# The output product of chunks 3 to 8 computed in seven products over two chunks

## The chip, the core and the metric

The kernel runs on one core of a Trainium2 chip. The metric is the device time of one execution in microseconds, from three timed runs; a further execution was profiled, and all rows below are from it. Engines are called as in the profile: PE (TensorE), DVE (VectorE), ACT (ScalarE), POOL (GpSimd), SP (SyncE, which only issues DMAs here).

## The reference

Windowed attention of 8 batches, 8 heads, 576 tokens and head size 64 (half of the heads see the last 32 keys, half every fourth of the last 128), then a feed-forward layer over all 4608 tokens:

```python
attn = exp(scores - max) / sum; x = (attn @ v) as 4608 x 512
h = x @ w_in                                   # 512 -> 2048
g = np.maximum(h, 0.0) + np.log1p(np.exp(-np.abs(h)))
return g @ w_out                               # 2048 -> 512
```

## The kernel before, in words

Tokens go in nine chunks of 512 (`CH`), the 2048 columns of the hidden layer in 16 tiles `ff` of 128, two neighbouring tiles being an ff pair `p` (eight pairs). Every fp32 operand is cut into a high part (an ACT cast) and a low part (a DVE subtraction), and a product is three matmuls: high by high, high by low, low by high. All stand at line 205, one 128x512 matmul each.

Chunks 0 to 2 are computed plainly (`h_part`, `o_part`). Chunks 3 to 8 go in three doubles `d` of two chunks. Their first layer is already done in seven products over two chunks: `combine` and `split_*` make blocks a11, a12, a22, s1 to s4 of x, `weights_of_pair` makes combined weights t1 to t4 beside b11, b21, b22, and for each pair `product` issues seven products of six matmuls into two PSUM banks `h_x` and `h_y` in turn. After each product `aside` takes the bank out: a plain copy (L1342) or an addition to an earlier sum (L1344). A product may begin when the aside two products earlier has read its bank. The sum for one tile and one chunk is a unit: Abs, Exp, Ln on ACT (L1354 to L1360), softplus on DVE (L1364), cast on ACT (L648), subtraction on DVE (L654), each 128x512. The second layer is plain: `late_o` takes one unit and adds it with three matmuls each into four banks o0 to o3, 12 matmuls for a unit, so 16 x 2 x 12 = 384 for a double, beside 8 x 7 x 6 = 336 of the first layer. The last unit of all is done in halves of 256 columns, so that its evacuation and its DMAs can begin early.

Attention of a later chunk runs beside: 28 visits of PE (`visit`, tile `sv_ps`), each followed by masking, maximum, eight Exp on ACT, division and a transposition through DRAM.

The order of instructions on each engine is made when the program is built: a list scheduler holds tasks with a cost and dependencies. PE has two lists, `first` (products of h) and `second` (output matmuls); `choose` takes a product once `upto` output tasks are done, and the other list where the wanted one is not ready. The other engines take the ready task of the least rank. `tc.keep_in_program_order` pins the outcome, so each engine works its list strictly in that order.

Of the kernel before, what the change touches and what calls it, by code (L numbers as in the profile page):

```python
# [23 lines left out]
DM, DF = 512, 2048  # L24
# [26 lines left out]
EARLY = 2  # L51
HANDED = 22
VISIT_EVERY = 14.0
# [45 lines left out]
def tile_windowed_attention_softplus_ffn(  # L99
# [16 lines left out]
    dpool = ctx.enter_context(tc.tile_pool(name="dec", bufs=3))  # L116
    psum = ctx.enter_context(tc.tile_pool(name="psum", bufs=2, space=bass.MemoryType.PSUM))

    consts = const.tile([P, P + 2 * SW], BF16, name="consts")
# [45 lines left out]
    def decode_step(ff, i, step):  # L165
        key = ff, i
        if step == 0:
            words[key] = raws[key].bitcast(I32).rearrange("p (n t) -> p n t", t=2)
            words[key] = (*(words[key][:, :, j] for j in range(2)), dpool.tile([P, DM], F32, name="a"))
# [63 lines left out]
    def scratch(shape, name, c, pr):  # L233

        if c == 0:
            tag = idle.pop(0)
        elif c == 1:
            tag = turns[name][pr % len(turns[name])]
        else:
# [4 lines left out]
    still = const.tile([P, CH], BF16, name="still")  # L244
    nc.gpsimd.memset(still, 0.0)

    def load_mask(c):
# [5 lines left out]
        masks[c] = wk.tile([P, 2 * SW], BF16, name="mask", bufs=2)  # L253
# [11 lines left out]
    x_full, ones, blocks = {}, {}, {}  # L265
# [7 lines left out]
    def split_x(c, k, low):  # L273
# [10 lines left out]
        "a11": ("xl10", "xl11"), "a12": ("xh10", "xh11"), "s2": ("w6_1", "w7_1"),  # L284
        "s3": ("w8_1", "w9_1"), "s1": ("w10_1", "w11_1"), "a22": ("w12_1", "xh00"),
        "s4": ("xh01", "xl00"),
    }

    def raw_block(d, name, kt):

        c = FIRST + 1 + 2 * d
        if name == "s1":
            if (d, kt) not in ones:
                if d == 0:
                    ones[d, kt] = const.tile([P, CH], F32, name="sums", tag=("g_x", "g_y")[kt])
                else:
                    if d not in ones:
                        ones[d] = const.tile([P, 2, CH], F32, name="sums", tag="w14_0")
                    ones[d, kt] = ones[d][:, kt]
            return ones[d, kt]  # L300
        half, k = {
            "a11": (0, 0), "s2": (0, 0), "a12": (0, 1), "s4": (0, 1),
            "a21": (1, 0), "s3": (1, 0), "a22": (1, 1),
        }[name]
        return x_half(c + half, k)[:, kt]

    def combine(d, name, kt):
# [6 lines left out]
            out=raw_block(d, name, kt), in0=raw_block(d, a, kt), in1=raw_block(d, b, kt), op=op  # L314
        ))

    def split_high(d, name, kt):
# [4 lines left out]
        pin(nc.scalar.copy(out=blocks[name][0][:, kt], in_=raw_block(d, name, kt)))  # L322

    def split_low(d, name, kt):
        high, low = blocks[name]
        pin(nc.vector.tensor_tensor(
            out=low[:, kt], in0=raw_block(d, name, kt), in1=high[:, kt].bitcast(F32),
            op=ALU.subtract,
# [298 lines left out]
    def activated(i):  # L627
        e = wk.tile([P, CH], F32, name="e")
# [11 lines left out]
    def g_tile(part, i):  # L640
        turn = i % 2 if i < len(slots) else i % 3
        return const.tile(
            [P, CH], F32R, name=f"g{part}", tag=f"g_{'xy'[part == 'l']}" if turn == 2 else f"g{part}{turn}"
        )

    def g_high(i, copy=None):
        gh = g_tile("h", i)
# [3 lines left out]
    def g_low(i):  # L651
        e, gh = ready[i]
        gl = g_tile("l", i)
# [4 lines left out]
    w_out = dram.tile([NFF, P, 2, DM], F32, name="w_out")  # L658
# [98 lines left out]
    sums, diffs, homes, thirds = {}, {}, {}, {}  # L757
# [3 lines left out]
    w_2 = dram.tile([NPAIR, P, 2, HALF], F32, name="w_2")  # L761

    def weight_sum(p, j):

        parts = wt[2 * p + j, 0].bitcast(F32)
        if p < EARLY:
            sums[p, j] = dpool.tile([P, 2, HALF], F32, name="b", tag="a")
        else:
            if j == 0:
                sums[p] = const.tile([P, 2, 2, HALF], F32, name="b", tag="x_a")  # L770
            sums[p, j] = sums[p][:, j]
        pin(nc.gpsimd.tensor_tensor(
# [968 lines left out]
```

## Time and profile before

| | before |
|---|---|
| median of 3 runs (lowest, highest) | 863.24 us (861.31, 868.94) |
| profiled execution: time, span | 866.28 us, 864.5 us |
| mean granted TensorE clock | 0.99 of full speed |
| PE, DVE, ACT, POOL busy | 98%, 65%, 63%, 7% |
| DMA | 173.87 MB, mean 201 GB/s |

The span runs from the first to the last instruction; 1.78 us of the profiled time lie outside it. Busy time of PE is of pipelined matmuls whose ends are modelled, so the distance between starts tells a matmul's cost, not its duration.

### The profile page before, as it was taken

How to read it: one execution, taken by the hardware profiler on the slowest of the kernel's cores; microseconds unless marked ns; L12 is line 12 of the kernel's file. 1: busy time of each engine (PE TensorE's matmuls, PEld its weight loads, DVE VectorE, ACT ScalarE, POOL GpSimd, SP SyncE). 2: the span in 40 equal slices, each digit the busy share in tenths (PEclk: the TensorE clock that was granted, in tenths of full speed). 3: DMA queues.
4: the chain of work that ended last, by engine and by line, in shares of the span. 5: the costliest groups of instructions: out<-in, count | busy, mean ns of one | idle time of the engine just before them, and what ended most of it. 6: DMA issues, size and time to landing. Idle time of an engine off the chain costs nothing.

```text
span 864.5 us, 20007 instructions
## 1 busy us (share of the span) xinstructions
PE 848.7 (98%) x7997; PEld 692.5 (80%) x7997; DVE 565.0 (65%) x950; ACT 548.5 (63%) x1354; POOL 59.5 (7%) x58
## 2 busy tenths in 40 slices
PE   7899989999999999999999999999999999999998
PEld 3688877888888888888888888888888888888886
DVE  5889878946464478788878646667685256556522
ACT  6888768776666576777777636777584256565521
POOL 0000000001111002245200000000000000000000
PEclk7999989999999999999999999999999999999999
DMA  7888823376886423788864875878644525662152
GB/s 254 262 264 276 289 81 132 118 247 247 282 328 223 133 88 125 244 284 272 288 218 149 266 253 176 253 245 269 207 134 157 194 101 188 177 206 74 57 193 92
DMA packets 90621, 173.87 MB, mean 201 GB/s; under 512 B 10016, under 2 KB 26528, under 8 KB 90528
## 3 DMA queue, kind: packets, MB, share of 16 engines
q1 hardware_dynamic: 90240, 172.19, 60.6%
q8 instruction: 63, 1.03, 0.5%
q10 hardware_dynamic: 288, 0.41, 0.1%
q14 instruction: 30, 0.25, 0.1%
HBM read 130.61 MB, written 41.94 MB: 200 GB/s over the span
## 4 chain that ended last, share of the span: by engine, by line
PE 89%; DMA 6%; ACT 2%; DVE 2%; issue 0%; SPq 0%; ACTq 0%
PE o_ps L205 44%; PE h_ps L205 14%; PE h_y L205 13%; PE h_x L205 13%; PE sv_ps L205 6%; DMA raw<-w 1%; DMA v<-vp 1%; DMA turned<-squares 1%; ACT s L437 1%; DMA pt<-turned 1%; DMA k<-kdl 1%; PE a_ps L205 0%; DMA mask<-cst 0%; DMA q<-qp 0%; DVE gl L654 0%
## 5 line engine op out<-in xcount | busy, mean ns | idle before, releaser
L205 PE MATMUL o_ps<-gh,t 128*128 128x512 f32 (+1 forms) x776 | 263.7, 389 | 0.0
L205 PEld LDWEIGHTS o_ps<-gh,t 128*128 128x128 f32 x776 | 145.2, 188 | 29.8
L205 PE MATMUL o_ps<-gl,t 128*128 128x512 f32 (+1 forms) x388 | 150.4, 388 | 0.2 <-DVE gl L654 0.2
L205 PE MATMUL h_ps<-xh,parts 128*128 128x512 f32 x384 | 131.7, 398 | 0.4 <-DVE e L636 0.4
L205 PE MATMUL o_ps<-gh,parts 128*128 128x512 f32 x384 | 130.3, 394 | 0.5 <-ACT ob L695 0.5
L205 PEld LDWEIGHTS o_ps<-gh,parts 128*128 128x128 f32 x384 | 72.6, 189 | 16.6 <-ACT ob L695 1.0
L205 PEld LDWEIGHTS h_ps<-xh,parts 128*128 128x128 f32 x384 | 72.6, 189 | 16.4 <-DVE e L636 0.9
L205 PEld LDWEIGHTS o_ps<-gl,t 128*128 128x128 f32 x388 | 72.9, 188 | 15.1 <-DVE gl L654 0.6
L437 ACT ACTIVATE s<-s,nm 128x64 f32<-128x64 f32 x224 | 74.8, 337 | 5.3 <-DVE nm L426 4.3
L648 ACT CAST gh<-stored 128x512 fp32r<-128x512 f32 x48 | 29.8, 621 | 72.1 <-PE o_ps L205 68.0
L205 PE MATMUL h_ps<-xl,parts 128*128 128x512 f32 x192 | 75.3, 392 | 0.0
L205 PE MATMUL o_ps<-gl,parts 128*128 128x512 f32 x192 | 75.3, 392 | 0.0
L654 DVE TENSOR_TENSOR gl<-stored,gh 128x512 fp32r<-128x512 f32 x48 | 33.0, 690 | 64.1 <-ACT gh L648 64.1
L1360 ACT ACTIVATE e<-e 128x512 f32<-128x512 f32 x96 | 60.3, 630 | 2.5
L1357 ACT ACTIVATE e<-e 128x512 f32<-128x512 f32 x96 | 60.2, 630 | 2.3
L205 PE MATMUL h_y<-s,t 128*128 128x512 f32 x216 | 55.3, 391 | 0.0
L205 PE MATMUL h_x<-s,t 128*128 128x512 f32 x216 | 55.1, 390 | 0.0
L1354 ACT ACTIVATE e<-hs 128x512 f32<-128x512 f32 x48 | 30.3, 631 | 36.2 <-DVE hs L1342 31.2
L648 ACT CAST gh<-hs 128x512 fp32r<-128x512 f32 x48 | 29.8, 621 | 36.6 <-DVE hs L1364 31.8
L636 DVE SCALAR_TENSOR_TENSOR e<-h_ps,e 128x512 f32<-128x512 f32 x48 | 32.8, 685 | 27.3 <-ACT e L1091 23.4
L205 PEld LDWEIGHTS h_y<-s,t 128*128 128x128 f32 x216 | 40.3, 188 | 8.8 <-DVE hs L1342 0.4
L205 PEld LDWEIGHTS h_x<-s,t 128*128 128x128 f32 x216 | 40.5, 188 | 8.5
(113 smaller groups left out, 1428.4 us busy)
## 6 DMA issues: line engine op xcount, KB each, us to landing
t<-w_out SPq DMA_DIRECT2D x132, 256.0 KB, 3.6
raw<-w SPq DMA_DIRECT2D x64, 256.0 KB, 4.3
v<-vp SPq DMA_DIRECT2D x28, 512.0 KB, 5.3
q<-qp SPq DMA_DIRECT2D x36, 256.0 KB, 4.2
w_out<-parts SPq DMA_DIRECT2D x16, 512.0 KB, 4.2
out_t<-ob SPq DMA_DIRECT2D x32, 256.0 KB, 3.2
t<-w SPq DMA_DIRECT2D x16, 512.0 KB, 3.8
turned_over<-w_one SPq DMA_DIRECT2D x16, 512.0 KB, 3.9
```

The source lines that it names most:

```text
L205: return tc.keep_in_program_order(nc.tensor.matmul(**kw))
L437: pin(nc.scalar.activation(out=self.blocks[:, t], in_=src, func=AF.Exp, bias=self.nm[:, t : t + 1], scale=1.0 / 8.0 if self.masked else 1. ...
L636: pin(nc.vector.scalar_tensor_tensor(out=e, in0=tiles.pop(i), scalar=0.0, in1=e, op0=ALU.max, op1=ALU.add))
L648: pin((copy or nc.scalar.copy)(out=gh, in_=ready[i]))
L654: pin(nc.vector.tensor_tensor(out=gl, in0=e, in1=gh.bitcast(F32), op=ALU.subtract))
L1354: pin(nc.scalar.activation(out=es[u], in_=ready[LATE + u], func=AF.Abs))
L1357: pin(nc.scalar.activation(out=es[u], in_=es[u], func=AF.Exp, scale=-1.0))
L1360: pin(nc.scalar.activation(out=es[u], in_=es[u], func=AF.Ln, bias=1.0))
```

## The change

The second layer of a double is now done in seven passes over all eight pairs (`PASSES`), each with one block of g (a11, a22, a12, s2, s1, s3, s4) and one combination of `w_out`. A step (`block_step`) is one pass for one pair: six matmuls into two banks. A double has 7 x 8 = 56 steps, 336 matmuls. For this, g is held in tiles of 128x1024 (`raw_g`: one of the two tiles ff of two neighbouring pairs, for one chunk): Abs, Exp, Ln and softplus work on these, DVE makes the sums s1 to s4 in place (`combine_g`), ACT and DVE cut each block into high and low (`block_high`, `block_low`) in one of two or three buffer sets; a set is refilled when the two steps that read it are done. At the end of a pass `put` moves the banks out, adding an earlier one on DVE where there is one.

Also: plain copies of the first layer's banks go from DVE to ACT (`aside`). The combined weights of both layers are made before the doubles, their sums on DVE and their differences on POOL. The weights of `w_out` are stored in DRAM as the passes want them (`w_o`) and streamed back in DMAs of 512 KB, 28 for each double. Some steps of the passes a11 and a22 are wanted among the 56 products of h by `due`; where a product is not ready, a step may come early. The last 16 steps of a double are wanted among the first products of the next one. Visits are at least 11 us apart while more than 16 are left, then 14 as before.

The core of the diff:

```diff
--- before.py
+++ after.py
+SPILL = 16
...
+DUE = 25
+APART = 3.5
...
+PASSES = (
+    ("a11", "b11", 0, True), ("a22", "t4", 1, True), ("a12", "b21", 0, False), ("s2", "t2", 1, True),
+    ("s1", "t1", 0, True), ("s3", "t3", 1, False), ("s4", "b22", 0, False),
+)
 HANDED = 22
-VISIT_EVERY = 14.0
+VISIT_EVERY = 11.0
...
+    a_tiles = [const.tile([P, DM], F32, name="a", tag=f"a{k}") for k in range(5)]
...
+    def g_set(n, dtype=F32R):
+        if (n, dtype) not in g_sets:
+            g_sets[n, dtype] = [const.tile([P, 2, CH], dtype, name="g", tag=f"g{n}{k}") for k in range(2)]
+        return g_sets[n, dtype]
...
+    def weight_sum(i, p, j):
+
+        parts = wt[2 * p + j, i].bitcast(F32)
+        sums[i, p, j] = in_turn_tile().rearrange("p (k n) -> p k n", k=2)
+        pin(nc.vector.tensor_tensor(
+            out=sums[i, p, j].rearrange("p k n -> p (k n)"), in0=parts[:, 0], in1=parts[:, 1], op=ALU.add
+        ))
...
+    def take(out, in0, in1):
+        pin(nc.gpsimd.tensor_tensor(out=out, in0=in0, in1=in1, op=ALU.subtract))
...
     def aside(dst, b, temp=None):
         if temp is None:
-            pin(nc.vector.tensor_copy(out=dst, in_=banks[b]))
+            pin(nc.scalar.copy(out=dst, in_=banks[b]))
         else:
             pin(nc.vector.tensor_tensor(out=dst, in0=banks[b], in1=temps(temp), op=ALU.add))
...
+    def late_softplus(key):
+        h = raw_g(*key)
         pin(nc.vector.scalar_tensor_tensor(
-            out=h, in0=h, scalar=0.0, in1=es.pop(u), op0=ALU.max, op1=ALU.add
+            out=h, in0=h, scalar=0.0, in1=es.pop(key), op0=ALU.max, op1=ALU.add
         ))
...
-    def late_o(u, m, half=None):
-        c, ff = uses[u]
-        gh, gl = ready[LATE + u]
-        begins, final = u % NFF == 0, u % NFF == NFF - 1
-        if begins:
-            o_ps[m] = bank(f"o_ps{m}", f"o{m}")
-        cols = slice(0, CH) if half is None else slice(half * HALF, (half + 1) * HALF)
-        ws = slice(m * P, (m + 1) * P)
-        for j, (part, gg) in enumerate(((0, gh), (0, gl), (1, gh))):
-            matmul(
-                out=o_ps[m][:, cols], lhsT=held[ff][:, part, ws], rhs=gg[:, cols],
-                start=begins and j == 0, stop=(final or u == len(uses) - 2) and j == 2,
-                skip_group_check=half is not None,
-            )
-
...
+    def combine_g(name, c):
+        a, b, op = SUMS[name]
+        pin(nc.vector.tensor_tensor(
+            out=raw_g(c, *PLACE[name]), in0=raw_g(c, *PLACE[a]), in1=raw_g(c, *PLACE[b]), op=op
+        ))
+
+    def block_high(k, name, c):
+        pin(nc.scalar.copy(out=set_of(k)[0], in_=raw_g(c, *PLACE[name])))
+
+    def block_low(k, name, c):
+        high, low = set_of(k)
+        pin(nc.vector.tensor_tensor(
+            out=low, in0=raw_g(c, *PLACE[name]), in1=high.bitcast(F32), op=ALU.subtract
+        ))
+
+    def set_of(k):
+        return blocks["s4"] if k == 2 else g_set(k)
+
+    obank = {}
...
+    def block_step(d, i, p, k):
+        x, w, b, begins = PASSES[i]
+        gh, gl = (part[:, p % 2] for part in set_of(k))
+        tile_of = stream[d, i, p // 2]
+        for m in range(2):
+            if begins and p == 0:
+                obank[b, m] = bank(f"o_ps{2 * b + m}", f"o{2 * b + m}")
+            for j, (part, gg) in enumerate(((0, gh), (0, gl), (1, gh))):
+                matmul(
+                    out=obank[b, m], lhsT=tile_of[:, p % 2, part, m * P : (m + 1) * P], rhs=gg,
+                    start=begins and p == 0 and j == 0, stop=p == NPAIR - 1 and j == 2,
+                    skip_group_check=not begins,
+                )
+
...
+    def put(name, m, b, other=None):
+        dst = held_tile(name, m)
+        if other is None:
+            pin(nc.scalar.copy(out=dst, in_=obank[b, m]))
+        else:
+            pin(nc.vector.tensor_tensor(out=dst, in0=obank[b, m], in1=held_tile(other, m), op=ALU.add))
...
+    in_turn = [(i, c) for c in range(COUPLES) for i in (0, 1)]
+    in_turn += [(i, c) for i in range(2, len(PASSES)) for c in range(COUPLES)]
+
+    def due(d, n):
+
+        return sum(14 * c + DUE + APART * j <= n for c in range(3) for j in range(4))
...
+                n = len(steps) * p + k
+                base = given + 2 * len(in_turn) * d
+                if d == 0:
+                    task.upto = min(base, given - 2 * NKT + n)
+                else:
+                    task.upto = base - SPILL + min(n, SPILL)
+                task.upto += due(d, n)
...
+                at_n = len(steps) * (NPAIR * d + p) + k
+                task.deps.append(asides.get(at_n - 2) or plus_done[46 + k])
...
+                mine = asides[at_n] = Task(
+                    f"aside {d} {p} {k}", ACT if temp is None else DVE, 0.62 if temp is None else 0.70,
+                    emit, [task, before],
+                )
...
+            k = (turn - 8) % 3 if 7 < turn < 20 else turn % 2
...
+            high = Task(f"high {d} {x} {c}", ACT, 1.07, lambda k=k, x=x, c=c: block_high(k, x, c), [raw, *set_deps])
+            low = Task(f"low {d} {x} {c}", DVE, 1.24, lambda k=k, x=x, c=c: block_low(k, x, c), [high])
+            block_done[d, x, c] = low
+            for p in (2 * c, 2 * c + 1):
+                step = Task(
+                    f"step {d} {x} {p}", PE, 6 * MM, lambda d=d, i=i, p=p, k=k: block_step(d, i, p, k),
+                    [low, Landed((d, i, c))],
+                )
...
```

How the order moves, at three places. In the rows, h_x and h_y are the banks of the first layer, o_ps those of the second, a_ and s_ the blocks of x, t the weights.

PE among the products of the second double, before: after each product come output matmuls, three to a bank.

```order
L205 MATMUL h_x<-s_4282,t_3507 128x512
L205 MATMUL h_x<-s_4283,t_3507 128x512
L205 MATMUL h_x<-s_4282,t_3507 128x512 x2
L205 MATMUL h_x<-s_4283,t_3507 128x512
L205 MATMUL h_x<-s_4282,t_3507 128x512
L205 MATMUL o_ps_6931<-gh,t 128x512
L205 MATMUL o_ps_6931<-gl,t 128x512
L205 MATMUL o_ps_6931<-gh,t 128x512
L205 MATMUL o_ps_6956<-gh,t 128x512
L205 MATMUL o_ps_6956<-gl,t 128x512
L205 MATMUL o_ps_6956<-gh,t 128x512
```

The same place after the change: two products stand behind each other, and a step comes after them.

```order
L233 MATMUL h_x<-s_4420,t 128x512
L233 MATMUL h_x<-s_4421,t 128x512
L233 MATMUL h_x<-s_4420,t 128x512 x2
L233 MATMUL h_x<-s_4421,t 128x512
L233 MATMUL h_x<-s_4420,t 128x512
L233 MATMUL h_y<-a_4378,t 128x512
L233 MATMUL h_y<-a_4379,t 128x512
L233 MATMUL h_y<-a_4378,t 128x512 x2
L233 MATMUL h_y<-a_4379,t 128x512
L233 MATMUL h_y<-a_4378,t 128x512
L233 MATMUL o_ps_6765<-g,t 128x512 x3
L233 MATMUL o_ps_6769<-g,t 128x512 x3
```

What moved: the next product into a bank now often has one product between it and the last one into that bank, and nothing else.

DVE among the products of the first double, before: rows L1344 and L1342 take a bank out, and what stands between them is 128x512.

```order
L1364 SCALAR_TENSOR_TENSOR hs<-hs,e 128x512
L1344 TENSOR_TENSOR stored<-h_x,temps 128x512
L654 TENSOR_TENSOR gl<-hs,gh 128x512
L1344 TENSOR_TENSOR stored<-h_y,temps 128x512
L1364 SCALAR_TENSOR_TENSOR stored<-stored,e 128x512
L1344 TENSOR_TENSOR hs<-h_x,temps 128x512
L1364 SCALAR_TENSOR_TENSOR stored<-stored,e 128x512
L1342 COPY temps<-h_y 128x512
L1364 SCALAR_TENSOR_TENSOR hs<-hs,e 128x512
```

After, where L1376 takes a bank out, L1397 is softplus and L1412 a sum of g:

```order
L1376 TENSOR_TENSOR stored<-h_x,temps 128x512
L1397 SCALAR_TENSOR_TENSOR stored<-stored,e 128x1024 x2
L1412 TENSOR_TENSOR stored<-stored 128x1024
L1376 TENSOR_TENSOR temps<-h_x,temps 128x512
L1412 TENSOR_TENSOR stored<-stored 128x1024 x2
L1376 TENSOR_TENSOR a<-h_x,temps 128x512
L1376 TENSOR_TENSOR stored<-h_y,a 128x512
L1397 SCALAR_TENSOR_TENSOR stored<-stored,e 128x1024
L1376 TENSOR_TENSOR stored<-h_x,temps 128x512
```

What moved: instructions of 128x1024 now stand ahead of rows that take a bank out.

DVE between the products of the first double and those of the second, where PE works on the second layer, before: the low parts of the stored units and one group of attention.

```order
L449 TENSOR_SCALAR sm<-sm 128x8
L452 RECIPROCAL ri<-sm 128x8
L455 TENSOR_TENSOR s<-s,ri 128x512
L654 TENSOR_TENSOR gl<-stored,gh 128x512
L477 STREAM_TRANSPOSE squares<-s 128x512
L654 TENSOR_TENSOR gl<-stored,gh 128x512 x4
L415 SCALAR_TENSOR_TENSOR s<-sv_ps,mask 128x512
L426 TENSOR_REDUCE nm<-s 128x8
```

After, at the same place (L1421 a low part of g, L1459 a bank of a pass):

```order
L1412 TENSOR_TENSOR stored<-stored 128x1024
L1421 TENSOR_TENSOR s_4550<-stored,s_4549 128x1024
L1421 TENSOR_TENSOR g<-stored,g 128x1024
L1459 TENSOR_TENSOR a<-o_ps_4957,ob 128x512
L1397 SCALAR_TENSOR_TENSOR stored<-stored,e 128x1024
L1459 TENSOR_TENSOR a<-o_ps_4961,ob 128x512
L468 TENSOR_SCALAR sm<-sm 128x8
L471 RECIPROCAL ri<-sm 128x8
L474 TENSOR_TENSOR s<-s,ri 128x512
L496 STREAM_TRANSPOSE squares<-s 128x512
L1421 TENSOR_TENSOR g<-stored,g 128x1024 x2
```

What moved: softplus and the sums of the last pairs, low parts of 128x1024 and additions out of the banks now stand here together.

## Rows read from the trace of the kernel before

**Rows 1.** The page's first part: busy time of an engine (share of the span), instructions.

```profile
PE 848.7 (98%) x7997; PEld 692.5 (80%) x7997; DVE 565.0 (65%) x950; ACT 548.5 (63%) x1354; POOL 59.5 (7%) x58
```

**Rows 2.** Stretches of the span: length, then busy time (and instructions) of PE, PEld, DVE, ACT and POOL, granted clock, DMA share, GB/s.

```profile
225.00:250.00 25.00, 25.00 (x231) 20.58 (x230) 14.03 (x25) 17.54 (x55) 1.70 (x1) 1.00 0.93 313
...
400.00:425.00 25.00, 25.00 (x229) 20.30 (x228) 21.69 (x34) 17.23 (x45) 13.71 (x12) 1.00 0.83 284
...
440.00:466.00 26.00, 26.00 (x235) 21.43 (x234) 23.04 (x39) 21.70 (x50) 0.00 (x0) 1.00 0.47 145
...
600.00:625.00 25.00, 24.53 (x195) 20.21 (x189) 17.76 (x28) 14.93 (x37) 0.00 (x0) 1.00 0.69 204
```

**Rows 3.** The waits of PE: who waited for whom, us in total, times, longest.

```profile
PE sv_ps L205 <- DMA pt<-turned: 3.0, 3, 1.4
...
PE o_ps L205 <- DVE gl L654: 0.2, 1, 0.2
```

**Rows 4.** The chain of work that ended last, in order of time: start, us, what.

```profile
602.13 2.78 ACT s L437 x16
...
661.92 40.80 PE o_ps L205 x180
```

**Rows 5.** Groups by line and form on PE: the output matmuls of the doubles (busy us, mean ns of one, idle before).

```profile
L205 PE MATMUL o_ps<-gh,t 128*128 128x512 f32 x760 | 260.8, 391 | 0.0
L205 PE MATMUL o_ps<-gl,t 128*128 128x512 f32 x380 | 148.1, 390 | 0.2 <-DVE gl L654 0.2
```

**Rows 6.** Groups by line and form on DVE (busy us, mean ns of one, idle before): low part and softplus of a stored unit, a plain aside, and the one form of 128x1024.

```profile
L654 DVE TENSOR_TENSOR gl<-stored,gh 128x512 fp32r<-128x512 f32 x48 | 33.0, 690 | 64.1 <-ACT gh L648 64.1
L1364 DVE SCALAR_TENSOR_TENSOR stored<-stored,e 128x512 f32<-128x512 f32 x48 | 32.9, 690 | 3.2 <-ACT e L1360 3.1
...
L1342 DVE COPY hs<-h_x 128x512 f32<-128x512 f32 x12 | 8.3, 691 | 5.9 <-PE h_x L205 5.4
...
L277 DVE TENSOR_TENSOR xl<-x_full,xh 128x1024 fp32r<-128x1024 f32 x2 | 2.3, 1201 | 0.0
```

**Rows 7.** The same view for ACT: one pass of Exp, a copy out of a PSUM bank, the one form of 128x1024.

```profile
L1357 ACT ACTIVATE e<-e 128x512 f32<-128x512 f32 x96 | 60.2, 630 | 2.3
...
L1116 ACT COPY ob<-o_ps 128x512 f32<-128x512 f32 x12 | 7.0, 586 | 12.1 <-PE o_ps L205 12.0
...
L281 ACT CAST xh<-x_full 128x1024 fp32r<-128x1024 f32 x2 | 2.1, 1040 | 0.0
```

**Rows 8.** The same view for POOL: a difference of combined weights.

```profile
L780 POOL TENSOR_TENSOR t<-b 128x256 f32<-128x256 f32 x8 | 7.5, 934 | 4.4 <-DVE a L326 2.9 <-DVE t L792 1.0
```

**Rows 9.** Timeline of DVE where nothing is waited for: start us, duration us, line, operation.

```profile
465.18 0.68 DVE L326 TENSOR_TENSOR s<-sums,s 128x512 fp32r<-128x512 f32 x1
465.79 0.68 DVE L326 TENSOR_TENSOR a<-x_full,a 128x512 fp32r<-128x512 f32 x1
466.39 0.68 DVE L654 TENSOR_TENSOR gl<-hs,gh 128x512 fp32r<-128x512 f32 x1
```

**Rows 10.** Timeline of PE and DVE where the kernel before has four products behind each other: the first three, and the aside of the first.

```profile
656.32 1.52 PE L205 MATMUL h_x<-a,turned_over 128*128 128x512 f32 x6
...
657.67 1.52 PE L205 MATMUL h_y<-s,t 128*128 128x512 f32 x6
...
657.88 0.69 DVE L1342 COPY hs<-h_x 128x512 f32<-128x512 f32 x1
...
659.03 1.52 PE L205 MATMUL h_x<-s,t 128*128 128x512 f32 x6
```

**Rows 11.** Timeline of POOL and DVE where both work on tiles in SBUF.

```profile
387.56 2.51 POOL L772 TENSOR_TENSOR b<-parts 128x512 f32<-128x512 f32 x2 [2.50 <-DVE parts L792]
...
388.84 1.79 DVE L1364 SCALAR_TENSOR_TENSOR hs<-hs,e 128x512 f32<-128x512 f32 x1
```

**Rows 12.** Stretches with the columns of rows 2, around PE's longest pause after the opening, and one of much DMA before it.

```profile
100.00:106.00 6.00, 6.00 (x29) 4.95 (x27) 5.77 (x11) 3.99 (x9) 1.52 (x1) 1.00 1.03 381
...
114.00:116.00 2.00, 2.00 (x31) 1.74 (x28) 1.09 (x2) 0.00 (x0) 0.00 (x0) 0.50 0.58 146
116.00:118.00 2.00, 2.00 (x6) 1.52 (x6) 1.93 (x5) 0.28 (x1) 0.00 (x0) 0.50 0.62 236
118.00:120.00 2.00, 2.00 (x7) 1.57 (x6) 0.74 (x2) 1.94 (x4) 0.00 (x0) 0.60 0.00 0
```

**Rows 13.** Timeline of PE: the waits of that pause, and the longest one after it, in brackets.

```profile
111.25 0.30 PE L205 MATMUL sv_ps<-pt,v 64*64 64x32 f32 x4 [1.12 <-DMA pt<-turned]
...
112.91 1.92 PE L205 MATMUL sv_ps<-pt,v 64*64 64x32 f32 x60 [1.36 <-DMA pt<-turned]
...
615.69 1.12 PE L205 MATMUL sv_ps<-pt,v 64*64 64x32 f32 x60 [0.47 <-DMA pt<-turned]
```

**Rows 14.** The end of the timeline: the last evacuation and the last DMA (its issue).

```profile
860.66 0.42 DVE L1616 COPY pt<-o_ps 128x256 f32<-128x256 f32 x1 [0.29 <-PE o_ps L205]
...
861.12 0.34 SPq L1622 DMA_DIRECT2D out_t<-pt  x1
```

**Rows 15.** The page's part on DMA issues: count, KB each, median us from issue to landing.

```profile
out_t<-ob SPq DMA_DIRECT2D x32, 256.0 KB, 3.2
```

More of the change, by code (lines that the diff above doesn't have):

```diff
@@ L788, in high_part, with weight_24 @@
+    def weight_24(i, p):
+        d, one, two = diffs[i, p], sums[i, p, 0], sums[i, p, 1]
+        take(two[:, 1], two[:, 1], d[:, 0])
+        b21 = one[:, 1] if i == 0 else two[:, 0]
+        take(b21 if i == 0 and p < RESIDENT else two[:, 0], b21, two[:, 1])
     def high_part(high, low, src):
@@ new lines, in tile_windowed_attention_softplus_ffn, with feed @@
+    stream, spare, tag_of = {}, [], {}
+    saved = set()
+    wanted = []
+    def feed(tag):
+        spare.append(tag)
+        begun = []
+        while spare and (key := wanted[0]()) is not None:
+            d, p, what = key
+            assert key in saved or all((*key, j) in saved for j in range(2)), key
+            tag_of[key] = spare.pop(0)
+            tile_of = stream[key] = const.tile([P, 2, 2, HALF], F32R, name="t", tag=tag_of[key])
+            if what == "2":
+                load_dma(out=tile_of[:, 0].bitcast(F32), in_=w_2[p])
+                begun.append((key, 0.256))
+                continue
+            src = {
+                "one": lambda: w_one[p].rearrange("p a (b n) -> p a b n", b=2),
+                "two": lambda: w_two[p].rearrange("p a (b n) -> p a b n", b=2),
+                "13": lambda: w_13[p],
+            }.get(what, lambda: w_o[p, what])()
+            load_dma(out=tile_of.bitcast(F32), in_=src)
+            begun.append((key, 0.512))
+        return begun
@@ L881, in add_buffer @@
[L881 to L893 removed]
+        both = home(p) if d == 0 and p < RESIDENT else tile_of
@@ L895, in visit @@
+        return [[both[:, part, h, k * P : (k + 1) * P] for k in range(2)] for part in range(2)]
     def visit(n, alone=False):
@@ L1014, in open @@
                 self.after <= t + 1e-9
[L1015 removed]
+                and all(
+                    d.over(t + LATENCY * (getattr(d, "engine", PE) == self.engine != PE)) for d in self.deps
+                )
                 and all(ring.open(t) for ring, _ in self.takes)
@@ new lines, in run @@
+    def run(task, t, engine=PE):
+        for ring, until in task.takes:
+            ring.take(until)
+        task.emit()
+        cost = task.cost
+        if engine == DVE and cost > 0.40 and not task.name.startswith(FROM_PSUM):
+            cost += min(max(free_at[POOL] - t, 0.0), SHARED)
+        if task.engine == SP:
+            free_at[SP] = t + 0.08
+            task.end = arrival(t, task.cost)
+        else:
+            free_at[task.engine] = t + cost
+            task.end = t + cost + LATENCY + 0.2 * (task.engine == PE)
+        heapq.heappush(ends, task.end)
+        heapq.heappush(ends, free_at[task.engine])
+        if engine in queues:
+            queues[engine].remove(task)
```

1092 lines of the change are left out of this document (558 added, 534 removed), and 4 rows, old and new, of the table s3.

## The prediction

> **What bounds the kernel now.** I read the page's first part first [rows 1]: PE is busy for 98% of the span, DVE and ACT for about two thirds, POOL for 7%. A mean over stages can hide a stage with another limit, so the stretches come next [rows 2]: while DMA is at 93%, while POOL works for 55% of the stretch and DVE for 21.69 of 25 us, and while DVE (23.04 of 26) and ACT are both loaded, PE has no idle time. Then the waits of PE [rows 3]: the largest group from 8 us to the end is 3.0 us, for attention's data, and the output matmuls waited 0.2 us in all. The chain of waits agrees [rows 4]: its long links are PE's own work, 180 output matmuls in 40.80 us, so 0.2267 us for one matmul. Work taken off PE therefore shortens the kernel, as long as what replaces it keeps clear of PE.
>
> **What PE saves.** The trace has 760 + 380 output matmuls of the doubles [rows 5], and 24 halves that count as 12: 1152. After the change there are 3 x 56 x 6 = 1008. Products of h (1008) and visits (28) stay. So 144 matmuls go, 144 x 0.2267 = 32.6 us, if PE is as full as before.
>
> **What the other engines get.** Counted from the order, priced by rows. DVE [rows 6]: 48 plain asides leave (48 x 0.69 = -33); 96 softplus of 0.69 become 48 of 1.20 (-9); 96 low parts of 0.69 become 84 of 1.20 (+34); 48 sums of g come (+58), 36 additions out of banks (+25); weight sums move here from POOL (32 x 0.69, +22), and low parts of weights add some 10; plain evacuations that leave give -7. Together about +98: 565 + 98 = 663 us, 79% of a span of 841. The form of 128x1024 is priced by its one row, 1.20. ACT [rows 7]: 48 copies at 0.586 (+28), casts of 84 x 1.04 for 96 x 0.63 (+27), Abs, Exp and Ln on 1024 columns instead of twice 512 (144 x (1.04 - 1.26) = -32), weight casts a few: about +30, 578 us, 69%. POOL: 64 differences at 0.93 [rows 8], 60 us, all ahead of the doubles' products. No engine is full on average; what matters is what stands behind what, since each works its list strictly in order.
>
> One thing decides how full DVE is. Where nothing is waited for, instructions that last 0.68 begin 0.61 and 0.60 apart [rows 9], so durations overcount its load by about a tenth. The Trainium skill, "VectorE: DVE Perf Modes", section on the DRAIN, says that the next instruction does not start until the pipe of the one before is empty; these starts disagree, though the same section allows that an instruction not held by a wait begins earlier. If the rule held throughout, DVE's load would be the durations in full; that is rival 2, worked out from rows.
>
> **Asides behind long instructions.** A product may begin once the aside two products earlier has read its bank. In the order, products whose predecessor into the same bank stands two back, with only one product between, go from 4 to 54 (the second excerpt of the order shows such a place). The row for this [rows 10]: products start 1.35 apart; the aside of the first ran from 657.88 to 658.57, 0.46 before the third product started into its bank. So an aside may be 0.46 late free of charge. In 25 of the 54 it stands directly behind a 128x1024 instruction (17 on DVE, 8 on ACT). If that has just begun, the aside comes 1.20 late and the product waits 0.74; if it is nearly over, nothing. With the moment of arrival evenly spread over the 1.20, the mean wait is 0.74 x 0.74 / (2 x 1.20) = 0.23 us. **25 x 0.23 = 5.7 us**, between 0 and 25 x 0.74 = 18.5. Behind a waiting product stands all of PE, its steps included.
>
> **POOL.** A softplus that ran beside a POOL sum took 1.79 instead of 0.69 [rows 11], so removing that work beside the doubles gives DVE some time, which nothing waited for: 0. The differences now beside the weights' preparation also slow DVE there; PE was full in such a stretch (400 to 425 in [rows 2]), so 0, at most 3.
>
> **DMA.** The order has 193 MB instead of 172. The heaviest intervals between visits carry 7232 KB in 21.2 us of matmuls (349 GB/s) and 5952 KB in 18.5 (330). Such rates have been met: 381 GB/s over 6 us with PE full [rows 12], and 313 over 25. I cost them at 0, upper end 5. Visits 11 us apart instead of 14 spread the same matmuls otherwise: 0.
>
> **Between the products of two doubles.** Here PE works steps only, and DVE must make low parts (1.20), puts, the last softplus and sums, and attention. By durations DVE has 57.7 us of this after the first double, in 240 matmuls and 3 visits of 2.0 (60.4 us of PE), and 54.3 in 58.4 after the second; by spacing a tenth less. It fits, with 2.7 to 8 us to spare. With 89% as the most DVE has shown beside a full PE (23.04 of 26 [rows 2]), it would need 65.1 and 61.3, so 7.6 us too much: the upper end. A set's refill takes 1.04 + 1.20 in sequence, 2.28 with gaps; two steps on another set cover 12 x 0.2267 = 2.72, and twice that where three sets turn. At the handover from pair 7's products to the steps that need them, ACT has seven instructions of 1.05, two casts of 1.04, eight Exp in 2.78 [rows 4], a copy of 0.59; with an aside and a low part 14.9 us, against ten products and a visit, 15.6. That is 0.7 to spare, three times. I take **2.0 us** for the stretches together, nearer to 0 because durations themselves still fit.
>
> A pause can cost more than itself. After PE waited 1.12 and 1.36 for a transposition [rows 13], the granted clock stood at 0.50, 0.50 and 0.60 in the next three stretches of 2 us [rows 12], 1.2 of 2.4 GHz: some 2.7 us lost on top. A pause of 0.47 [rows 13] left the stretch around it at 1.00 [rows 2]. My waits are of the second size, so no clock term. The Trainium skill, "TensorE: Matmul & The Clock Gate", also has an idle array at the lower rate until it has been busy again; this trace agrees, and by it short waits in sequence could add what rival 3 counts.
>
> **The end.** Before, the last half bank took 0.42 on DVE and its DMA began 0.04 later, 3.4 before the end [rows 14]. Now a whole bank is added (0.69) and 256 KB go out, whose landing took 3.2 in the median [rows 15]. **+1.1**, between 0.5 and 2.
>
> **Sum**, against the profiled span: 864.5 - 32.6 + 5.7 + 2.0 + 1.1 = 840.7. With 1.78 around it 842.5, beside 866.28 before. That execution is 3.04 above the median of the runs, so the median becomes 839.4, rounded to 839. With its own bounds (asides 0 to 12, stretches 0 to 5) this case runs from 832 to 848.
>
> **Rivals.** 1. All covered: DVE's starts as close as in [rows 9] everywhere and asides arriving in good time. 864.5 - 32.6 + 0.5 = 832.4, median 831. For it: PE lost 0.2 us at output matmuls so far. Against: 25 asides did not stand behind 1.20 before.
> 2. DVE bounds the step stretches, and DMA its busiest intervals: 7.6 for 2.0 and 3 for DMA, so 840.7 + 5.6 + 3 = 849.3, median 848. For it: each figure of DVE counted in durations leaves under 3 us. Against: the spacing.
> 3. Within 1%: the handovers, only 0.7 us to spare, become pauses of 2.5 us as large as that of [rows 13], each with 2.7 at half clock: 3 x 5.2 = 15.6, median 855. Against: ACT's chain there would have to slip by over 3 us, past the 0.7 to spare.
> 4. Slower: in the products DVE and ACT run a backlog, so that an aside always meets a 128x1024 instruction just begun. Each of the 54 tight products then waits 0.74, 40.0 in place of 5.7: median 874. It decides against the change from 40 of the 54 on (839.4 - 5.7 + 40 x 0.74 = 863.3). The order speaks against: only 25 stand directly behind one.
>
> **How the numbers follow.** About 1%, 8.6 us, can be told from no change here. Chances: the forecast 0.42, rival 1 0.20, rival 2 0.20, rival 3 0.11, rival 4 0.07. Faster by over 1% (under 854.6): 0.82; within 1%: 0.11; slower: 0.07. The range for 8 in 10 goes from 830, just under rival 1, to 854, over rival 2.
>
> **What the changed profile would show.** 1008 output matmuls of the doubles, a long run of them still 0.227 apart; else the saving is wrong. PE's waits behind products named by DVE or ACT lines of asides, some 6 us together, mostly under 0.74 each; none is rival 1, 40 is rival 4. DVE near 663 us and ACT near 578; waits of output matmuls for low parts in the step stretches about 2 us; more with DVE full there is rival 2. Stretches of granted clock under 1.00 in the doubles would be rival 3. Wrong altogether I would be if PE waited for streamed weights, which I cost at 0, or if a 128x1024 instruction of DVE took much over 1.20.

## The result, and the profile after

| | before | after |
|---|---|---|
| median of the runs (lowest, highest) | 864.51 us (861.31, 868.94; 4 runs, the profiled one among them) | 838.12 us (837.28, 839.28; 4 runs) |
| ratio to before, 95% interval | | 0.9692 [0.9645, 0.9740] |
| profiled execution: time, span | 866.28, 864.5 us | 839.28, 837.5 us |

The kernel is faster by 3.1%, within the stated range and 1 us from the forecast. A second set of six runs gave 838.55 us and 0.9691 [0.9656, 0.9727]. Three executions in the sets below, one of the kernel before and one each of the kernels with plain asides on DVE and with softplus in halves, ran at a mean granted clock of 0.59 to 0.85 and are left out of all medians and ratios.

The page's first part, to be read against [rows 1]: PE lost 33.5 us of busy time, DVE gained 89, ACT 29. PE is still the one engine without room on average.

```profile
PE 815.2 (97%) x7839; PEld 664.1 (79%) x7841; DVE 654.0 (78%) x923; ACT 577.6 (69%) x1235; POOL 63.6 (8%) x74
```

Groups by line and form on PE and then on DVE (busy us, mean ns of one, idle before). The second layer of the doubles is now 864 + 144 = 1008 matmuls where the kernel before had 1152 (the 1140 of [rows 5], and 24 halves that count as 12). The new forms of 128x1024 on DVE take 1.22 us, against 1.20 of the one row there was [rows 6].

```profile
L233 PE MATMUL o_ps<-g,t 128*128 128x512 f32 x864 | 209.4, 390 | 0.6 <-DVE g L1421 0.5
...
L233 PE MATMUL o_ps<-s,t 128*128 128x512 f32 x144 | 34.9, 390 | 0.0
```

```profile
L1421 DVE TENSOR_TENSOR g<-stored,g 128x1024 fp32r<-128x1024 f32 x72 | 87.7, 1220 | 33.2 <-ACT g L1417 32.9
L1412 DVE TENSOR_TENSOR stored<-stored 128x1024 f32<-128x1024 f32 x48 | 58.3, 1218 | 0.5
L1397 DVE SCALAR_TENSOR_TENSOR stored<-stored,e 128x1024 f32<-128x1024 f32 x48 | 58.2, 1216 | 2.5 <-ACT e L1393 2.4
```

To see where time went, both spans are cut where the first product of h starts. The two stretches of the kernel before, then of the one after (length, then busy time and instructions of PE, PEld, DVE, ACT and POOL, granted clock, DMA share, GB/s):

```profile
0.00:332.72 332.72, 321.45 (x3945) 257.63 (x3946) 232.85 (x423) 234.23 (x652) 25.95 (x28) 0.97 0.64 211
332.72:864.50 531.78, 527.27 (x4053) 434.85 (x4051) 332.15 (x529) 314.26 (x702) 33.56 (x30) 1.00 0.60 195
```

```profile
0.00:334.48 334.48, 317.81 (x3815) 255.89 (x3818) 262.55 (x464) 244.64 (x669) 63.55 (x74) 0.97 0.76 251
334.48:837.50 503.02, 497.43 (x4025) 408.26 (x4023) 391.40 (x460) 332.92 (x567) 0.00 (x0) 1.00 0.68 221
```

The second stretch is 28.8 us shorter. One visit moved into it from the first (128 matmuls of the small kind, 1.9 us), so 30.7 are gained there of the 32.6 of the 144 matmuls. The first stretch is 1.8 us longer, and 3.7 with the visit that left it. The second stretch came out the same in the second profile of this kernel, 503.15; the first one 332.35. In what follows "from the first product on" is this second stretch; 5.6 of its 503.0 us are idle on PE.

The waits of PE (us in total, times, longest):

```profile
PE sv_ps L233 <- DMA pt<-turned: 5.6, 5, 3.2
...
PE o_ps L233 <- DVE g L1421: 0.5, 1, 0.5
```

No wait for an aside is in that list, and none for streamed weights. Why no aside was late shows in the timelines of PE and DVE at the tightest place of the whole program:

```profile
704.50 1.52 PE L233 MATMUL h_x<-s,t 128*128 128x512 f32 x6
705.86 1.52 PE L233 MATMUL h_y<-a,t 128*128 128x512 f32 x6
707.22 1.52 PE L233 MATMUL h_x<-s,t 128*128 128x512 f32 x6
708.58 1.59 PE L233 MATMUL h_y<-a,t 128*128 128x512 f32 x6
```

```profile
706.06 0.69 DVE L1376 TENSOR_TENSOR stored<-h_x,a 128x512 f32<-128x512 f32 x1 [0.52 <-PE h_x L233]
706.67 1.22 DVE L1397 SCALAR_TENSOR_TENSOR stored<-stored,e 128x1024 f32<-128x1024 f32 x1
707.80 0.69 DVE L1376 TENSOR_TENSOR stored<-h_y,temps 128x512 f32<-128x512 f32 x1
```

The product into h_y starts at 705.86, the next into h_y at 708.58. The aside between stands behind a softplus of 1.22, begins at 707.80 and ends at 708.49, 0.09 before it is needed. A product that does have to wait starts about 0.06 behind its aside (366.95 and 367.01 in a run below), so only some 0.03 was left. The aside ahead of the softplus, at 706.06, had waited 0.52 for PE: DVE was there first. Over all 54 tight products, 46 asides end 0.46 us or more ahead of the product that waits for them, as the one of [rows 10] that nothing held up; 8 are held up by 0.04 to 0.37 (seven behind a 128x1024 instruction, one behind a 128x512 one of attention), and the smallest margin is this 0.09. One such narrow place is nothing new: the kernel before had a product that started 0.06 behind its aside, although output matmuls stood between its products.

```profile
421.48 0.68 DVE L1342 COPY hs<-h_y 128x512 f32<-128x512 f32 x1
...
422.22 1.65 PE L205 MATMUL h_y<-s,t 128*128 128x512 f32 x6
```

The end: the last two banks are evacuated together, and 3.4 us pass from there to the end of the span, as before [rows 14].

```profile
832.76 1.37 DVE L1459 TENSOR_TENSOR ob<-o_ps,ob 128x512 f32<-128x512 f32 x2 [2.45 <-PE o_ps L233]
```

### The profile page after: what moved, and what is told of

Same layout as the page of the kernel before. It is cut to its first block, busy times and chain, and to the rows that moved or that the text cites. A ratio compares the mean times of both kernels' runs of the same rounds, so it can differ in the third digit from the quotient of the medians.

```text
span 837.5 us, 19536 instructions
## 1 busy us (share of the span) xinstructions
PE 815.2 (97%) x7839; PEld 664.1 (79%) x7841; DVE 654.0 (78%) x923; ACT 577.6 (69%) x1235; POOL 63.6 (8%) x74
## 4 chain that ended last, share of the span: by engine, by line
PE 80%; DMA 7%; DVE 7%; ACT 4%; issue 1%; SPq 1%; ACTq 0%
PE o_ps L233 36%; PE h_x L233 13%; PE h_y L233 13%; PE h_ps L233 11%; PE sv_ps L233 5%; DMA pt<-turned 2%; ACT s L456 2%; DMA v<-vp 1%; DMA turned<-squares 1%; DMA q<-qp 1%; DVE a L217 1%; SPq L168 1%; DVE a L212 1%; DMA k<-kdl 1%; DMA raw<-w 1%
## 5 line engine op out<-in xcount | busy, mean ns | idle before, releaser
L233 PE MATMUL o_ps<-g,t 128*128 128x512 f32 x864 | 209.4, 390 | 0.6 <-DVE g L1421 0.5
L233 PEld LDWEIGHTS o_ps<-g,t 128*128 128x128 f32 x864 | 161.5, 188 | 35.2 <-DVE g L1421 1.6
L233 PE MATMUL o_ps<-g,parts 128*128 128x512 f32 x576 | 142.3, 393 | 0.7 <-ACT ob L707 0.6
L233 PEld LDWEIGHTS o_ps<-g,parts 128*128 128x128 f32 x576 | 107.1, 188 | 24.2 <-ACT ob L707 1.5
L1417 ACT CAST g<-stored 128x1024 fp32r<-128x1024 f32 x72 | 75.5, 1050 | 62.3 <-PE o_ps L233 55.6
L1421 DVE TENSOR_TENSOR g<-stored,g 128x1024 fp32r<-128x1024 f32 x72 | 87.7, 1220 | 33.2 <-ACT g L1417 32.9
L785 POOL TENSOR_TENSOR a<-a 128x256 f32<-128x256 f32 x64 | 56.9, 897 | 99.0 <-DVE a L780 83.4
L1397 DVE SCALAR_TENSOR_TENSOR stored<-stored,e 128x1024 f32<-128x1024 f32 x48 | 58.2, 1216 | 2.5 <-ACT e L1393 2.4
L1412 DVE TENSOR_TENSOR stored<-stored 128x1024 f32<-128x1024 f32 x48 | 58.3, 1218 | 0.5
L1390 ACT ACTIVATE e<-e 128x1024 f32<-128x1024 f32 x48 | 50.8, 1057 | 0.9
L1393 ACT ACTIVATE e<-e 128x1024 f32<-128x1024 f32 x48 | 50.6, 1059 | 1.0
```

What stands on the lines that cost most here:

```text
L233: return tc.keep_in_program_order(nc.tensor.matmul(**kw))
L785: pin(nc.gpsimd.tensor_tensor(out=out, in0=in0, in1=in1, op=ALU.subtract))
L1390: pin(nc.scalar.activation(out=es[key], in_=es[key], func=AF.Exp, scale=-1.0))
L1393: pin(nc.scalar.activation(out=es[key], in_=es[key], func=AF.Ln, bias=1.0))
L1397: pin(nc.vector.scalar_tensor_tensor(out=h, in0=h, scalar=0.0, in1=es.pop(key), op0=ALU.max, op1=ALU.add))
L1412: pin(nc.vector.tensor_tensor(out=raw_g(c, *PLACE[name]), in0=raw_g(c, *PLACE[a]), in1=raw_g(c, *PLACE[b]), op=op))
```

## The experiments

Two theories. A: PE alone sets the time, and what was gained is the 144 matmuls. B: DVE and ACT now stand so close behind PE that the order decides how much of the gain is kept. Ratios are to the kernel before on the same chip; the changed kernel has 0.969, and 1% is 8.6 us. The runs with a cost of 1.40 and with later visits had the changed kernel beside them on their chip; elsewhere two ratios are compared, each known to 2 to 5 us.

**More and fewer matmuls in the steps, in the same order.** A fourth matmul, low by low, in three of the seven passes:

```diff
+            parts = ((0, gh), (0, gl), (1, gl), (1, gh)) if i in (2, 3, 4) else ((0, gh), (0, gl), (1, gh))
```

> 144 matmuls more: a fourth matmul (low by low) for each bank in the steps of the passes a12, s2 and s1, in the order of the changed kernel otherwise. Theory, PE alone sets the time of the doubles and the 144 matmuls that the change took away are what it gained: 144 x 0.2267 = 32.6 us back, 870 to 872 us. Rival, DVE or ACT set the step stretches behind a PE that looks busy: there they gain time from longer steps, and less than 25 us come back.

865.95 us, ratio 1.0009 [0.9981, 1.0037]; from the first product on 534.70 us, 31.7 more than 503.02. There the whole gain is given back: A holds in this direction. The total missed the 870 to 872 of the theory; by the ratios 27.4 us came back, so that the total alone does not exclude the rival's 25. The difference lies ahead of the cut, where the order of both kernels is the same: this execution reached the first product of h at 330.10, the changed kernel's at 334.48. Then two matmuls instead of three in the same passes:

```diff
+            parts = ((0, gh), (0, gl)) if i in (2, 3, 4) else ((0, gh), (0, gl), (1, gh))
```

> 144 matmuls less: the steps of the passes a12, s2 and s1 leave out low weights by high g, so the output is less exact; order otherwise as in the changed kernel. Theory, PE alone bounds and the others have room: 32.6 us less, about 805. Rival, DVE is next close behind: after the first two doubles it has 57.7 and 54.3 us of work by durations where PE would then have 49.5 and 47.5, so 8.2 and 6.8 us of the 32.6 are not had and the time is about 820, with PE waiting for low parts of g.

819.78 us, ratio 0.9500 [0.9447, 0.9553]; from the first product on 489.64, only 13.4 less (16.6 in the total, by the ratios). The rival's 820 came out. The waits of PE name the engine, DVE with its low parts of g, where the changed kernel has 0.5 us:

```profile
PE o_ps L233 <- DVE g L1421: 10.4, 12, 1.8
...
PE o_ps L233 <- DVE s L1421: 1.5, 2, 1.3
```

In one of the stretches behind the second double's products (columns as above), DVE is busy without a gap and PE is not:

```profile
630.00:640.00 10.00, 8.23 (x32) 6.01 (x31) 10.00 (x11) 6.28 (x8) 0.00 (x0) 0.89 0.67 232
```

So with this order the changed kernel stands just short of the point at which DVE takes over: from the first product on, 32.6 us more on PE show nearly in full, 32.6 us less at 41%. The scheduler still counted six matmuls for the shortened steps. An order made for four was not tried, so how much of the missing 59% is DVE's load and how much the unfitting order is not separated.

**The same work, planned with wrong durations.** Only the cost that the scheduler is told changes, for DVE's and ACT's 128x1024 instructions of the doubles:

```diff
-Task(f"plus {name}", DVE, 1.24, ...)
+Task(f"plus {name}", DVE, 0.62, ...)
-Task(f"low {d} {x} {c}", DVE, 1.24, ...)
+Task(f"low {d} {x} {c}", DVE, 0.62, ...)
```

(and the sums, casts, Abs, Exp and Ln alike).

> The same work, but the list scheduler is told half the cost for each 128x1024 instruction of the doubles (0.62 and 0.54 to 0.58 instead of 1.24 and 1.07 to 1.16), so that it no longer knows which aside a long instruction will hold up. Theory, it is the order made with true costs that keeps the asides clear: PE now waits for asides, 3 to 18 us in all, 841 to 856. Rival, ACT and DVE simply have time to spare, in whatever order: within 1.5 us of 838.

909.46 us, ratio 1.0526 [1.0478, 1.0573]: slower than the kernel before, with the very instructions of the changed kernel, and far outside what either side expected. From the first product on 575.86 us, 72.8 more. The stretches and the waits of this kernel split that:

```profile
332.44:908.30 575.86, 524.52 (x4025) 411.23 (x4023) 393.58 (x460) 332.99 (x567) 0.00 (x0) 0.98 0.60 193
```

```profile
PE o_ps L233 <- DVE g L1421: 11.6, 8, 2.4
PE h_y L233 <- DVE temps L1376: 9.1, 7, 1.9
PE h_x L233 <- DVE a L1376: 5.5, 4, 1.7
PE h_x L233 <- ACT temps L1374: 5.1, 3, 2.1
PE h_y L233 <- DVE a L1376: 4.2, 4, 2.4
```

PE is idle for 575.86 - 524.52 = 51.3 us instead of 5.6, and its 4025 matmuls are busy 27.1 us longer. The first is mostly waits for low parts and asides (lines L1374, L1376). Of the second, the mean granted clock of 0.98 instead of 1.00 accounts for some 12 us (575.86 x 0.02). A matmul counts as busy for 0.39 us where the next can follow after 0.2267, so each of 43 waits in the list may hide up to 0.16 more; that estimate gives some 6 us, and the rest is not placed. One such wait, in ACT's timeline: a cast, Abs, Exp, Ln and the next Abs stand in front of a plain copy that PE needs.

```profile
364.48 1.06 ACT L1393 ACTIVATE e<-e 128x1024 f32<-128x1024 f32 x1
365.44 1.04 ACT L1387 ACTIVATE e<-stored 128x1024 f32<-128x1024 f32 x1
366.39 0.56 ACT L1374 COPY temps<-h_x 128x512 f32<-128x512 f32 x1
```

The copy ends at 366.95, and PE's product starts at 367.01 after 2.06 us of waiting. This is B, and stronger than I had put it: DVE and ACT have 22 and 31% of their time free in the changed kernel, yet an order made without true durations loses the whole gain and 45 us more. Too high a cost, 1.40 for DVE's 1.22, was tried too:

```diff
-Task(f"plus {name}", DVE, 1.24, ...)
+Task(f"plus {name}", DVE, 1.40, ...)
```

(and the low parts and sums alike).

> The scheduler is told 1.40 instead of 1.24 for each 128x1024 DVE instruction of the doubles (they take 1.22). Theory, asides are clear already and a margin moves little: within 2 us of the changed kernel. Rival, the order is so sensitive that a planner off by 13% loses several us, as being off by half lost 71: 4 us or more slower.

845.71 us, ratio 0.9777 [0.9750, 0.9804]: 7 us slower than the changed kernel beside it, the rival's result. The waits that are new are 4.1 us for low parts and a cast of g, each behind the last products of a double.

```profile
PE o_ps L233 <- DVE g L1421: 2.5, 3, 1.0
PE o_ps L233 <- ACT g L1417: 1.6, 1, 1.6
```

**No steps among the products.**

```diff
-SPILL = 16
+SPILL = 0
-DUE = 25
+DUE = 1000
```

> No step of a pass is wanted among the products of h any more (due never adds one, and the last 16 steps of a double are no longer kept for the next one); the scheduler may still take one where a product is not ready. Theory, mixing is what gives ACT and DVE the time to keep up with seven products a pair: in products alone ACT has about 80 us in 86 of PE for a double, and PE waits now and then for an aside: 3 to 8 us slower than the changed kernel, 841 to 846. Rival, mixing is worth nothing because the lists have room anyway: within 1.5 us of 838.

844.10 us, ratio 0.9766 [0.9721, 0.9811], about 6 us slower. From the first product on 511.32, 8.3 more; PE waited for low parts of g seven times, 3.5 us in all, and for asides four times, 1.1 us in all. The theory's size is right; its place only in part, since the low parts lost more than the asides, and some 3.7 of the 8.3 are not placed.

**Two buffer sets throughout.**

```diff
-k = (turn - 8) % 3 if 7 < turn < 20 else turn % 2
+k = turn % 2
```

> Two buffer sets for the blocks of g throughout, where turns 8 to 19 of a double had three. Theory, a refill of 1.04 + 1.20 behind another instruction of 1.20 on DVE is later than the 2.72 us of two steps by 0.76, and half of the 36 blocks meet one: 8 to 16 us slower, PE waiting for low parts of g. Rival, the refill of 2.28 fits in 2.72 and the third set is a luxury: within 1.5 us of 838.

843.99 us, ratio 0.9770 [0.9743, 0.9798]: about 6 us slower, less than the 8 to 16 of the theory. From the first product on 507.68, 4.7 more, of which waits for low parts are 1.9 in four pieces. So fewer refills than half were late, and the rest of the loss is not placed.

**Parts of the change undone on DVE, ACT and POOL.** Plain asides on DVE again:

```diff
-pin(nc.scalar.copy(out=dst, in_=banks[b]))
+pin(nc.vector.tensor_copy(out=dst, in_=banks[b]))
```

> The 48 plain copies out of the first layer's banks go back from ACT to DVE (+33 us on DVE, -28 on ACT), the order made anew with that known. Theory, the order keeps asides clear as long as DVE is not full in the products: within 3 us of 838. Rival, DVE at 78% is so near its bound that 4% more show: 5 to 15 us slower, with PE waiting for asides.

845.59 us (three runs), ratio 0.9801 [0.9752, 0.9850]: 9 us slower by the ratio, the rival's size. No trace that can be compared shows where it waited; the cause stays open. Softplus in two halves, planned with 1.38 instead of 1.24:

```diff
-out=h, in0=h, scalar=0.0, in1=es.pop(key), op0=ALU.max, op1=ALU.add
+out=h[:, j], in0=h[:, j], scalar=0.0, in1=e[:, j], op0=ALU.max, op1=ALU.add
```

> Softplus of the doubles in two instructions of 128x512 instead of one of 128x1024 (48 x (2 x 0.69 - 1.22) = 8 us more on DVE by durations), Abs, Exp and Ln still on 1024 columns. Theory, DVE has just enough room in the step stretches: within 2 us of 838. Rival, DVE is what bounds them already: 3 to 6 us slower.

840.03 us (three runs), ratio 0.9739 [0.9702, 0.9776]: 4 us slower by the ratio, at the edge of what can be told; from the first product on 509.45, 6.4 more. PE waited 2.3 us for low parts (0.5 in the changed kernel) and 0.4 for a cast, and its granted clock fell for a while at 448 (last section). Sums of the combined weights back on POOL:

```diff
-a = Task(f"sum0 {name}", DVE, 0.70, ...)
+a = Task(f"sum0 {name}", POOL, 1.6, ...)
```

> The 32 sums of combined weights go from DVE back to POOL (POOL +49 us, DVE -22), all before or early in the first double. Theory, nothing of that stage is on the path: within 1.5 us of 838. Rival, DVE's instructions beside POOL take up to 1.79 instead of 0.69 and the weights come later: 3 to 8 us slower.

844.97 us, ratio 0.9783 [0.9745, 0.9820]: 8 us slower. From the first product on 505.02, only 2.0 more; the rest is lost before. The first product of h itself waited:

```profile
PE h_x L233 <- DVE e L655: 3.9, 1, 3.9
```

It needs a bank that a plain softplus reads. DVE came to that at 338.64, behind four low parts of weights that it began at 333.64, after POOL's last four differences (329.35 to 332.43), and two instructions for x. Before these low parts DVE stood idle for 3.2 us, up to 331.09, for attention's Exp on ACT; the changed kernel fills that wait with its own last four low parts (324.93 to 327.42), whose differences are ready by then. So the rival's size came, and by POOL's lateness and the order made around it more than by slower DVE instructions; that is read from these times and was not tested by itself.

For the last five runs (no steps among the products, two sets, and the three here) the order was made anew. The run with 1.40 lost 7 us by a new order alone, with the same instructions. So how much of the 4 to 9 us lost here belongs to what was undone, and how much to an order that merely came out less well, these runs do not separate.

**Later visits.** After the change the largest wait on PE is for attention's data. The scheduler was told that it comes later:

```diff
             task.end = arrival(t, task.cost)
+            if task.name.startswith("bring"):
+                task.end += 4.0 if t < 30.0 else 1.0
```

The control beside it, the changed kernel:

> The changed kernel once more, beside the three others of this set. All theories: 838 within 2 us, 0.969 of the kernel before. If it comes out near 842, the differences of a few us that other runs showed against it are the spread from one chip to the next.

838.55 us, ratio 0.9691 [0.9656, 0.9727].

> The scheduler is told that a transposed block comes back from DRAM 1.0 us later than it thought, and the first one of the stage 4.0 us later, so that PE works longer on other products before a visit. Theory, the waits for this data (5.6 us in the changed kernel, with a granted clock of half behind the longest) can be filled: 3 to 6 us faster than the changed kernel beside it. Rival, later visits make the blocks of x later in turn and the wait only moves: within 1.5 us of it, or slower.

855.69 us, ratio 0.9892 [0.9862, 0.9921]: 17 us slower. The wait wasn't even filled, and a longer one came:

```profile
PE h_y L233 <- ACT s L342: 7.7, 1, 7.7
PE o_ps L233 <- DVE g L1423: 4.3, 5, 1.3
PE sv_ps L233 <- DMA pt<-turned: 3.2, 1, 3.2
```

The rival holds: later visits make the blocks of x for the first double later, and its second product waits 7.7 us for s, with the granted clock at 0.63 and 0.86 in the two stretches of 10 us from 340 on. With 2.0 and 6.0:

> As the run before, with 2.0 and 6.0 us. Theory, nothing is left to fill beyond the 3.2 us of the longest wait: the same as with 1.0 and 4.0 within 1.5 us. Rival, 28 visits a us later each starve the second double of x: 3 us or more slower than with 1.0 and 4.0.

853.51 us, ratio 0.9875 [0.9841, 0.9908], within the uncertainty of the run before: the long wait at 113 us is gone, but s is 10.3 us late. Neither of the two beat the changed kernel.

## Why the prediction was right, step by step

**What PE saves: right.** 1008 matmuls are there, the stretch from the first product on is 30.7 us shorter than its visits account for, and 144 matmuls put back cost 31.7. The 0.2267 us of [rows 4] was the right price.

**Asides behind long instructions: the term that failed.** I took 5.7 us, from an arrival "evenly spread over the 1.20". It was 0. The 54 tight products and the long instructions ahead of asides are as counted, but the arrival is not random: the order is made with durations close to the true ones, so that the long instruction has mostly ended when PE's bank is full (the 0.52 us for which DVE waited at 706.06, the 0.09 left at 708.49). The run with halved costs shows that the mechanism itself is real, some 30 us in waits for asides, so it is the order that keeps the term at 0 and not free time on DVE. The 25 asides directly behind a 128x1024 instruction are in the trace, 17 on DVE and 8 on ACT; seven were held up, by at most 0.37, where 0.46 were free. Rival 4 was this mechanism; what I said against it, that only 25 asides stand directly behind one, was not the reason that it stayed away.

**Between the products of two doubles: right, at the low end.** 0.5 us of waits for low parts against 2.0 of 0 to 7.6. Durations did fit. Beside a full PE, DVE now reaches 19.17 of 20 us, past the 89% that I had used as an upper bound:

```profile
620.00:640.00 20.00, 20.00 (x209) 16.47 (x208) 19.17 (x21) 17.50 (x34) 0.00 (x0) 1.00 0.73 212
```

In the run with fewer matmuls it had no gap from 630 to 640, and PE waited. Rival 2 was thus near in the engine it named and wrong for this kernel's time.

**The end: 1.1 taken, about 0.2 measured.** From the last matmuls' modelled end to the end of the span are 4.1 us (833.40 to 837.5) against 3.9 before (860.63 to 864.5). Larger banks and DMAs cost little there.

**DMA: right at 0.** There is no wait for streamed weights in this kernel (three of the kernels with another order have 0.3 to 0.7 us). The first row has 349 GB/s beside a full PE, while the combined weights are made; the weights of the passes stream in from 348.84 on, and the second row is of such a stretch:

```profile
300.00:320.00 20.00, 20.00 (x209) 16.49 (x208) 16.07 (x27) 13.53 (x35) 9.52 (x12) 1.00 0.96 349
517.00:538.00 21.00, 21.00 (x213) 17.29 (x212) 14.29 (x20) 17.08 (x32) 0.00 (x0) 1.00 0.88 315
```

**Visits: 0 was too low.** The order built with 14 instead of 11 us between visits is the same row for row, so that this edit alone does nothing. But visits' data was late more often: 5.6 us of waits instead of 3.0 [rows 3], 0.9 of it at 450, in the second stretch, where the kernel before had 0.5 [rows 13]. The wait at about 112 us took 3.2 and 0.5 us here against 1.1 and 1.4 before [rows 13]. The time of the first product of h varies: 327.4 to 335.2 us in profiles of kernels whose order is the same up to there (fewer matmuls, two sets), so how much of the 3.7 us lost in the first stretch belongs to the change stays open.

So the 1 us between forecast and result is partly luck. With the asides at 0, the stretches at 0.5 and the end at 0.2 the sum would be 832.6 in place of 840.7, rival 1's figure; the 837.5 measured has 3.7 us more before the first product and 0.4 more at visits, which I had costed at nothing, and 0.8 not placed. The mechanism was rival 1's, the total the forecast's. **DVE** was put at 663 us (its terms as listed add up to 100, not 98) and took 654, **ACT** at 578 and took 577.6. Rival 3's pauses did not occur in the doubles: the granted clock is 1.00 from the first product on.

## What to carry to other kernels

When work leaves the engine that bounds a kernel, price the saving by that engine's own spacing, then ask how much room is left on the engine that takes its place: here 30.7 of 32.6 us were had behind the first product, and of the next 32.6 only 13.4, in an order not made for them. A mean share of 78% says little about room in an engine that works a fixed list; the margins in front of the instructions that another engine waits for do. The smallest was near its limit before and after; what grew, from 4 to 54, is the number of places where a few tenths of a us decide. If an order is planned, the durations that the planner believes are part of the kernel: half of the true ones cost 71 us, 13% too much cost 7, and each other kernel whose order was made anew lost 4 to 17, which may in part be the new order itself.

## What the runs showed of the hardware

**A pause of about 2 us costs clock in some places and none in others.** I knew two sizes from the kernel before: 0.47, which left the clock at 1.00, and 2.5 us in two parts, which didn't. In the kernel planned with halved costs, one pause of 2.06 us ended at 367. The four stretches of 2 us around and behind it (columns as above):

```profile
366.00:368.00 2.00, 0.99 (x4) 0.86 (x5) 1.49 (x2) 1.97 (x4) 0.00 (x0) 1.00 0.25 75
368.00:370.00 2.00, 2.00 (x6) 1.54 (x6) 0.96 (x1) 2.00 (x3) 0.00 (x0) 0.54 0.20 56
370.00:372.00 2.00, 2.00 (x6) 1.20 (x5) 1.97 (x3) 2.00 (x3) 0.00 (x0) 0.60 0.00 0
372.00:374.00 2.00, 1.81 (x8) 1.17 (x8) 1.80 (x3) 1.39 (x2) 0.00 (x0) 1.00 0.00 0
```

The granted clock is near half, 1.2 of 2.4 GHz, for some 4 us, which loses about 1.7 us (2 x 0.46 + 2 x 0.40) on top of the 2.06. In the same trace a longer pause, 2.37 us up to 669.94, left the clock at 1.00:

```profile
668.00:670.00 2.00, 0.06 (x1) 0.06 (x1) 2.00 (x4) 0.43 (x1) 0.00 (x0) 1.00 0.70 182
670.00:672.00 2.00, 2.00 (x9) 1.65 (x10) 2.00 (x3) 0.00 (x0) 0.00 (x0) 1.00 0.42 158
```

In the kernel with fewer matmuls the stretch from 630 to 640, with a pause of 1.77 in it, shows 0.89 (above), while that from 450 to 460, with one of 1.52, shows 1.00:

```profile
450.00:460.00 10.00, 8.48 (x44) 6.44 (x52) 9.74 (x13) 9.97 (x21) 0.00 (x0) 1.00 0.76 233
```

With softplus in halves, the clock fell behind four pauses of 0.40, 0.76, 0.83 and 0.57 us between 440 and 447:

```profile
448.00:450.00 2.00, 2.00 (x20) 1.62 (x13) 1.94 (x4) 1.97 (x3) 0.00 (x0) 0.52 1.08 362
450.00:452.00 2.00, 2.00 (x7) 1.56 (x6) 2.00 (x3) 0.20 (x2) 0.00 (x0) 0.63 0.88 324
```

So the length of one pause does not tell whether clock is lost; what else decides is not shown by these runs. The Trainium skill, "TensorE: Matmul & The Clock Gate", section "What's actually happening", has an idle array at the lower rate until it is busy again; the stretches behind 2.06 and 1.77 agree, and those behind 1.52 and 2.37 show pauses that cost no clock.

**DVE's starts stay closer than its durations with 1024 columns too.** In the timeline of the changed kernel two instructions that last 1.22 begin 1.13 and 1.14 us ahead of the next:

```profile
702.59 1.22 DVE L1397 SCALAR_TENSOR_TENSOR stored<-stored,e 128x1024 f32<-128x1024 f32 x1
703.72 1.22 DVE L1421 TENSOR_TENSOR g<-stored,g 128x1024 fp32r<-128x1024 f32 x1
704.86 0.68 DVE L1376 TENSOR_TENSOR a<-h_y,temps 128x512 f32<-128x512 f32 x1
```

The overlap is 0.08 to 0.09 us for each instruction, as in [rows 9] with 512 columns (0.07 to 0.08), so a smaller share of a longer instruction. I had taken a tenth for all of DVE's load; for these forms it is 7%.
